# Stores of a last batch issued per 32 rows over two queues, with a new instruction order

## The chip, the core and the metric

The kernel runs on one core of a Trainium2 chip. The metric is the device time of one execution in microseconds, as the median of five executions. A profiled execution gives, beside its own time, the span from its first to its last instruction; what lies between the two is outside the instructions. Engines: TensorE (PE) multiplies matrices and writes to the banks of PSUM; VectorE (DVE) and ScalarE (ACT) copy, add and apply functions; GpSimd (POOL) issues the loads here; SyncE (SP) issues transposing transfers and stores. ScalarE can issue stores too.

## The reference

An attention of the Nyström kind (8 batches, 8 heads, 576 tokens, 64 wide, 32 landmarks), and on its result, as 4608 tokens of 512 values, two dense layers with SiLU between them (2048 inner values):

```python
q_lm = q.reshape(B, H, m, S // m, D).mean(axis=3)      # m = 32 landmarks
k_lm = k.reshape(B, H, m, S // m, D).mean(axis=3)
A, Bm, C = sm(q, k_lm), sm(q_lm, k_lm), sm(q_lm, k)    # scaled softmaxes
Z = Bm.T / (norm(Bm, 1) * norm(Bm, inf) + 1e-06)
for _ in range(6):
    Z = 2 * Z - Z @ Bm @ Z
x = A @ Z @ C @ v                                       # then (B*S, H*D)
...
h = x @ w_in
g = h * (1.0 / (1.0 + np.exp(-h)))
return g @ w_out
```

## The kernel before

**Work of one batch.** The name of an operation ends in its batch (`A.3`). The kernel loads q, k and v of the batch (`ld`, `ldv`), transposes q and k (for batches 0 to 2 on TensorE, `tr` with copies `trc`; for later ones with four transposing transfers on SP, `xt`), and sums over the 18 positions of a landmark (`lms` on TensorE, or the VectorE tree `lra`, `lrb`, `lrc`, `lrd`). `sb` and `pb` make the small softmax, `ns0` to `ns5` on TensorE with `nsd0` to `nsd5` on VectorE the six iterations of the inverse. `A` is the softmax of q against the landmarks: scores `A`, exponentials `Ax`, sums `S`, reciprocals through `Ln` and `Rs`, product `etn`. `C`, `Cx`, `ct` (a transpose) and `cv` make C times v. `zt` multiplies with Z, and `m0` to `m3` multiply that with `w_in` at once, so that layer 1 is one small product, `etn` times `m`: sixteen tiles `h0` to `h15` of 512 tokens, each with a SiLU on ScalarE (`g0` to `g15`), and `hx0`, `hx8` with `gx0`, `gx8` for the 64 tokens left over of the batch. The SiLU needs another function table in ScalarE than the exponentials, and the kernel groups the two kinds.

**Layer 2** takes 256 tokens at a time (`layer2_pair`, from line 1027), in two halves of 128. The 2 x 2 blocks of tokens and columns are made with seven products instead of eight, as in Strassen's scheme: sums of blocks on VectorE (`ss0` to `ss3`), products `p1` to `p7` of eight matmuls each on TensorE, and copies (`c1`, `u2`, `c5`, `c21`) and additions (`c11`, `c22`, `c12`) that bring them into two tiles `ost` of the output, a low one and a high one, each of 128 tokens by 512 columns. Names carry a priority: `p1@5120` is batch 1 (5000 + 100 per batch), second pair (+ 20); + 40 is the pair that gathers the left-over tokens of four batches. The low tile is whole after `c11` (columns 0 to 255) and `c12` (256 to 511), the high one after `c21` and `c22`. There are six `ost` tiles in turn.

**Stores.** One tile of 128 rows is four blocks of 32 rows, which lie 18 rows apart in the output, so it leaves as four transfers (`store`, line 1021). Ordinarily one operation `os` on SP issues all four (line 1118). For the very last pair (`spread`, line 1108), the four stores of the low tile are four operations that SP or ACT may take, and the high tile is stored in eight halves of 256 columns, those of each half as soon as it is made.

**The order.** All is planned ahead: `Plan.run` (line 86) is a list scheduler. It keeps a time for each engine, takes the ready operation with the lowest priority, counts the costs and lags written in the code, and gives for every engine a fixed order of instructions, which the kernel then emits. Where TensorE would idle in the first 45 us of the plan, it issues a matmul on zeros (`P.filler`, line 497). Priorities may be shifted by the table `ORDER` (line 19), `name: (shift, not before)`, which was found by a search. The engines wait for one another through semaphores as the data need it; so an instruction that waits holds up all that stands behind it on its engine.

Of the kernel before, what the change touches and what calls it, by code (L numbers as in the profile page):

```python
# [16 lines left out]


ORDER = {
    "tr09.0": (11.858, 0), "f0.0": (2417.6, 0), "nsd20.0": (1178, 0), "stf1.0": (616.27, 0),  # L20
    "ns51.0": (572.47, 0), "A.0": (-14.244, 0), "Ax10.0": (-14.785, 0), "S10.0": (429.53, 0),
    "Ln10.0": (-9.5622, 0), "etn1.0": (303.1, 0), "mc00.0": (-3617.7, 0), "mc30.0": (2226.2, 0),
    "tr10.1": (11.49, 0), "trc09.1": (-0.41208, 0), "tr014.1": (4003.2, 0), "lms110.1": (600, 0),
    "lms1112.1": (182.03, 0), "lms006.1": (4219.8, 0), "ns00.1": (-205.63, 0),
    "Ax10.1": (-68.603, 0), "Ln10.1": (-2.9831, 0), "Ax11.1": (-215.55, 0),
    "Ln11.1": (-2436.1, 0), "Rs1.1": (-229.25, 0), "Cx00.1": (3739.9, 0), "ctc10.1": (-135.78, 0),
    "trc014.2": (-5.8828, 0), "Ln10.2": (-1553.1, 0), "Cx10.2": (-2.3811, 0), "h11.1": (3839, 0),
    "c12@5100.0": (-2978.9, 0), "A.3": (-178.57, 0), "cv0.3": (-11.245, 0), "h2.2": (332.83, 0),
    "h3.2": (185.78, 0), "h4.2": (18.041, 0), "h11.2": (452.76, 0), "h15.2": (51.328, 0),
    "p5@5200.0": (-179, 0), "c21@5200.0": (912.94, 0), "A.4": (-26.98, 0), "Ln00.4": (288.73, 0),  # L30
    "h11.3": (169.04, 0), "ss00@5320.0": (-3259.3, 0), "p5@5340.0": (-0.29183, 0),
    "p7@5340.0": (-4146.8, 0), "p3@5340.0": (212.88, 0), "nsd00.5": (-245.94, 0),
    "S10.5": (-942.67, 0), "p7@5420.0": (-0.18573, 0), "ns40.6": (267.98, 0),
    "ss00@5500.0": (-5226.2, 0), "cv0.7": (-3352.4, 0), "wrc.7": (1720.5, 0),
    "p5@5620.0": (-0.51334, 0), "p7@5700.0": (-1.908, 0), "p4@5720.0": (524.17, 0),
    "p2@5740.0": (15.37, 0),
}


# [272 lines left out]
def mm_us(n, count=1):  # L312
    return count * max(n / 2400 + 0.0025, 0.028)
# [3 lines left out]
def kernel(  # L317
# [10 lines left out]
    B, H, S, Dh = q.shape  # L328
# [31 lines left out]
    def bank(o, i=0):  # L360
        return banks[o.slot[i]]
# [33 lines left out]
    def mm(out_ap, lhsT, rhs, start=True, stop=True):  # L395
        nc.tensor.matmul(out=out_ap, lhsT=lhsT, rhs=rhs, start=start, stop=stop,  # L396
                         skip_group_check=True)
# [6 lines left out]
    def copy(e, out, in_):  # L404
        if e == "ACT":
            nc.scalar.copy(out=out, in_=in_)  # L406
        elif e == "DVE":
            nc.vector.tensor_copy(out=out, in_=in_)  # L408
        else:
            nc.gpsimd.tensor_copy(out=out, in_=in_)  # L410

    P = Plan()
    A = P.add

    def either(n, act=True, dve=True):
        r = []
        if dve:
            r.append(("DVE", dve_us(n)))
        if act:
            r.append(("ACT", act_us(n)))  # L420
        return r
# [512 lines left out]
    l2_last = {}  # L934
# [56 lines left out]
    ost_st = {}  # L991

    def layer2_plain(gm, c, deps, places, prio):

        pieces = []
        for h in range(2):
            cell = {}
            cols = slice(c + 128 * h, c + 128 * h + 128)
            for qt in range(4):
                def f(e, qt=qt, cell=cell, cols=cols):  # L1000
                    for dc in range(4 * qt, 4 * qt + 4):
                        mm(bank(cell["o"]), gm[:, dc, cols], w_out_sb[:, dc, :], start=(dc == 0),
                           stop=(dc == NDC - 1))
                d = deps(4 * qt, 4 * qt + 4) + [wo_ops[qt]]
                o = A(f"o{qt}@{prio + h}", [("PE", mm_us(512, 4))], f,
                      d + ([(pieces[-1], 0.0)] if qt else []), prio + h + 0.01 * qt,
                      psum=0 if qt else 1, cls="L2")
                cell.setdefault("o", o)
                pieces.append(o)
            i = nost[0] % 6  # L1010
            nost[0] += 1
            t = ost_r[i]
            a = A(f"oc@{prio + h}", either(512), lambda e, t=t, cell=cell: copy(
                e, t, bank(cell["o"])), [pieces[-1]] + ost_st.get(i, []),
                500.0 + prio / 100).reads(cell["o"])
            ost_st[i] = [A(f"os@{prio + h}", [("SP", 2.2)],
                           lambda e, t=t, h=h: [store(e, t, places[h], m) for m in range(4)],
                           [a], prio, dma=0.65, lag=3.5)]
        return pieces

    def store(e, t, place, m, cols=slice(0, DMODEL)):
        b, j = place[m]
        {"SP": nc.sync, "ACT": nc.scalar}[e].dma_start(
            out=out[b * S:(b + 1) * S, cols].rearrange("(l j) n -> j l n", j=J)[j],
            in_=t[L * m:L * m + L, cols])

    def layer2_pair(gm, c, deps, places, prio, parts=1, spread=False):

        n = npair[0]
        npair[0] += 1  # L1030
# [8 lines left out]
        for u in range(parts):  # L1039
            k = slice(w * u, w * u + w)  # L1040
            dep = deps(w * u, w * u + w) + deps(HC + w * u, HC + w * u + w) + ss_last.get(n - 2, [])
            for i, (o_, x, y, op) in enumerate((
# [6 lines left out]
                dep = [a]  # L1049
# [24 lines left out]
        def evac(nm, engs, f, deps, *of):  # L1074
            c = A(f"{nm}@{prio}", engs, f, deps, 500.0 + prio / 100)
            for o in of:
                c.reads(o)
            return c

        def add(out_, x, y):  # L1080
            nc.vector.tensor_tensor(out=out_, in0=x, in1=y, op=OP.add)  # L1081
# [3 lines left out]
        def ps(o):  # L1085
            return bank(o)[:, 0:HM]
# [3 lines left out]
        p2 = prod("p2", 1, a12, b21, [p1] + deps(HC, NDC) + w2)  # L1090
        c1 = evac("c1", half, lambda e: copy(e, lo_t[:, 0:HM], ps(p1)), [p1] + lo_free, p1)
        c11 = evac("c11", dve, lambda e: add(lo_t[:, 0:HM], lo_t[:, 0:HM], ps(p2)), [p2, c1], p2)
        p6 = prod("p6", 2, s2, wt[:, 1], [c1] + sums[2] + wts[1], p1)
        u2 = evac("u2", half, lambda e: copy(e, lo_t[:, HM:DMODEL], ps(p1)), [p6], p1)
        p5 = prod("p5", 3, s1, wt[:, 0], [p1] + sums[0] + wts[0])
        p7 = prod("p7", 4, a21, b12, [u2] + sums[1] + wts[3], p1)
# [3 lines left out]
        p3 = prod("p3", 5, s4, b22, [c5] + sums[3] + w2, p5)  # L1100
        p4 = prod("p4", 6, a22, wt[:, 2], [c22] + wts[2], p1)
        c12 = evac("c12", dve, lambda e: add(lo_t[:, HM:DMODEL], lo_t[:, HM:DMODEL], ps(p5)),
                   [p3, u2], p5)
        c21 = evac("c21", half, lambda e: copy(e, hi_t[:, 0:HM], ps(p1)), [p4], p1)
        ss_last[n] = [p3, p5, p6]

        for i, t, h, dep in ((lo_i, lo_t, 0, [c11, c12]), (hi_i, hi_t, 1, [c21, c22])):
            if spread and h:
                ost_st[i] = [A(f"os{u}{m}@{prio + h}", [("SP", 0.45), ("ACT", 0.45)],
                               lambda e, m=m, t=t, u=u: store(e, t, places[1], m, slice(  # L1110
                                   HM * u, HM * u + HM)), [dep[u]], prio + 0.1 * u,
                               dma=0.1, lag=1.5) for u in range(2) for m in range(4)]
            elif spread:
                ost_st[i] = [A(f"os{m}@{prio}", [("SP", 0.45), ("ACT", 0.45)],
                               lambda e, m=m, t=t: store(e, t, places[0], m), dep, prio,
                               dma=0.1, lag=1.5) for m in range(4)]
            else:
                ost_st[i] = [A(f"os@{prio + h}", [("SP", 2.2)],
                               lambda e, t=t, h=h: [store(e, t, places[h], m) for m in range(4)],
                               dep, prio, dma=0.65, lag=3.5)]  # L1120
        return pieces

    def layer2_batch(b):
        l2_last["m", b] = []
        for p in range(2):
            x = (gm_r[b % 2], 256 * p, lambda d0, d1: gm_ops[b][d0:d1],
                 [[(b, j) for j in range(8 * c + p, 8 * c + p + 7, 2)] for c in range(2)],
                 5000.0 + 100 * b + 20 * p)
            if b or p:
                l2_last["m", b] += layer2_pair(*x)  # L1130
            else:
                l2_last["m", b] += layer2_plain(*x)
                w_sums(l2_last["m", b][:])
        if b % 4 == 3:
            l2_last["x", b // 4] = layer2_pair(
                gx_t, 0, lambda d0, d1: [gx_ops[x][d // 8] for x in range(b - 3, b + 1)
                                         for d in range(d0 // 8 * 8, d1, 8)],
                [[(x, j) for x in (y, y + 1) for j in (J - 2, J - 1)] for y in (b - 3, b - 1)],
                5000.0 + 100 * b + 40, 1, b == B - 1)

    def later_loads(b):
        p = last[b - 2]
# [6 lines left out]
    for b in range(B + 1):  # L1149
        if b < B:  # L1150
            attn(b)
        if b:
            layer1(b - 1)
            layer2_batch(b - 1)
# [53 lines left out]
```

## Time and profile before

| | us |
|---|---|
| five executions | 249.02, 249.9, 249.63, 249.32, 249.56 |
| median | 249.56 |
| the profiled execution | 249.02 |
| its span | 247.3 |
| TensorE busy | 239.0 |
| VectorE, ScalarE busy | 168.7, 180.8 |
| last matmul ends, from the span's start | 242.6 |

The chain of waits and the groups of instructions name lines of the kernel; line 396 is the helper that emits every matmul, 406 and 408 are the copies on ScalarE and VectorE, 958 the SiLU, 1046 the sums of layer 2, 1081 its additions, 1023 a store. A row of a group has the number of instructions, busy time, mean duration of one in ns, and the idle time of the engine before them with what ended it. A matmul's duration overlaps the next one's, so starts tell more than durations. In the timeline a row has start, length, engine, line, what is written from what, the number of instructions merged, and in brackets the idle time before it. The stores' group of the page, with the number of issues, size of one, and the median from issue to landing:

```profile
out_dram<-ost SPq DMA_DIRECT2D x138, 64.0 KB, 1.8
out_dram<-ost SPq DMA_DIRECT2D x4, 32.0 KB, 1.5
out_dram<-ost ACTq DMA_DIRECT2D x4, 32.0 KB, 1.6
out_dram<-ost ACTq DMA_DIRECT2D x2, 64.0 KB, 1.8
```

### The profile page before, as it was taken

Reading aid. Unit: us, or ns where it says so; the run is one execution under the profiler, and the core shown is the slowest. Engines: PE = TensorE matmul, PEld = TensorE weight load, DVE = VectorE, ACT = ScalarE, POOL = GpSimd, SP = SyncE. Lnnn points to the kernel's source line nnn. Section 1 sums busy time; section 2 is a strip of 40 time slices with the busy share of each in tenths; the row PEclk is TensorE's granted clock in tenths of the full one; section 3 lists DMA queues with packets and bytes.
Section 4 is the critical chain, followed back from the end, with each engine's and each line's share of the span. In section 5 each row is a group of like instructions: output and inputs, shape, how many; then the busy total and the mean of one; then the engine's idle time right before and its main releaser. Section 6 shows DMA issues by size and latency. Waiting matters only on the chain.

```text
span 247.3 us, 7085 instructions
## 1 busy us (share of the span) xinstructions
PE 239.0 (97%) x2780; PEld 171.2 (69%) x2780; DVE 168.7 (68%) x432; ACT 180.8 (73%) x443; POOL 37.2 (15%) x63
## 2 busy tenths in 40 slices
PE   7999999999989999999999999999999999999992
PEld 5786664556867645577886645697885665788881
DVE  2379765495979947939998787099988365056620
ACT  2596997499776999999359998868667998831220
POOL 8436823300022004000310050000000000000000
PEclk9999999999999999999999999999999999999999
DMA  6999999999999999989899999884354003032332
GB/s 102 195 203 197 203 207 206 207 242 166 187 133 217 183 136 185 221 140 175 155 248 205 180 175 222 149 148 83 89 120 107 0 3 85 3 85 67 96 95 85
DMA packets 55680, 36.50 MB, mean 148 GB/s; under 512 B 36576, under 2 KB 47072, under 8 KB 55648
## 3 DMA queue, kind: packets, MB, share of 16 engines
q0 software_dynamic: 15264, 18.35, 44.5%
q1 hardware_dynamic: 40096, 17.45, 33.3%
q8 instruction: 21, 0.34, 0.5%
q10 hardware_dynamic: 288, 0.26, 0.4%
q14 instruction: 11, 0.09, 0.1%
HBM read 36.70 MB, written 9.44 MB: 187 GB/s over the span
## 4 chain that ended last, share of the span: by engine, by line
PE 88%; DMA 5%; DVE 2%; ACT 2%; issue 1%; POOL 0%; SPq 0%; DVEq 0%; POOLq 0%
PE ps L396 85%; DMA qk<-in_q_dram 3%; PE ps L570 2%; DMA qT<-qk 2%; ACT gm L958 1%; DMA out_dram<-ost 1%; DVE red L630 1%; PE ps L846 1%; POOL qk L449 0%; DVE ost L1081 0%; DVE ss L1046 0%; DVE gm L1046 0%; ACT pb L695 0%; ACT gx L981 0%; DVE st L756 0%
## 5 line engine op out<-in xcount | busy, mean ns | idle before, releaser
L396 PE MATMUL ps<-etn,m 128*128 128x64 bf16 (+1 forms) x512 | 69.5, 286 | 0.6 <-ACT gm L958 0.6
L958 ACT ACTIVATE gm<-ps 128x512 f16<-128x512 f32 x128 | 66.8, 658 | 1.3 <-PE ps L396 1.1
L396 PEld LDWEIGHTS <-gm 128*128 128x128 f16 x512 | 48.6, 98 | 11.4 <-issue 2.7
L396 PE MATMUL ps<-w_out_sb,gm 128*128 128x256 f16 (+1 forms) x392 | 53.1, 281 | 0.0
L396 PEld LDWEIGHTS <-m 128*128 128x128 bf16 x512 | 32.2, 98 | 24.3 <-issue 2.7
L406 ACT COPY ost<-ps 128x256 f32<-128x256 f32 (+1 forms) x55 | 21.2, 388 | 37.1 <-PE ps L396 34.6
L396 PEld LDWEIGHTS <-ss 128*128 128x128 f16 x408 | 38.8, 98 | 7.8 <-issue 2.3
L1081 DVE TENSOR_TENSOR ost<-ost,ps 128x256 f32<-128x256 f32 x51 | 21.3, 418 | 31.0 <-PE ps L396 24.4
L396 PE MATMUL ps<-wt,ss 128*128 128x256 f16 x272 | 34.3, 273 | 0.7 <-DVE ost L1081 0.7
L756 DVE SCALAR_TENSOR_TENSOR st<-st,ps 128x320 bf16<-128x320 bf16 (+3 forms) x54 | 21.7, 406 | 7.7 <-PE ps L396 6.7
L408 DVE CAST m<-ps 128x512 bf16<-128x512 f32 x31 | 20.1, 686 | 3.5 <-PE ps L396 3.5
L406 ACT CAST m<-ps 128x512 bf16<-128x512 f32 x33 | 18.2, 618 | 1.5 <-PE ps L396 1.4
L396 PE MATMUL ps<-w_out_sb,ss 128*128 128x256 f16 x136 | 17.6, 273 | 0.0
L455 POOL DMA_DIRECT2D qk<-in_k_dram x7 | 5.0, 714 | 79.8 <-DMA ct<-ce 41.4
L462 POOL DMA_DIRECT2D v<-in_v_dram x24 | 14.0, 590 | 15.7 <-PE ps L396 8.8
L396 PE MATMUL ps<-zer 128*128 128x256 bf16 x88 | 15.2, 298 | 1.1 <-DVE zer L489 1.1
L396 PE MATMUL ps<-wt,gm 128*128 128x256 f16 x120 | 15.6, 273 | 0.0
L831 ACT ACTIVATE ce<-ps 128x288 bf16<-128x288 f32 x32 | 12.7, 418 | 3.2 <-PE ps L396 3.2
L396 PE MATMUL ps<-st 128*128 128x160 bf16 (+1 forms) x96 | 14.6, 225 | 0.1
L1046 DVE TENSOR_TENSOR ss<-gm 128x1024 f16<-128x1024 f16 x15 | 10.2, 683 | 4.9 <-ACT gm L958 4.9
L796 ACT ACTIVATE ln<-ps 128x288 f32<-128x288 f32 x32 | 12.0, 433 | 1.8 <-PE ps L396 1.6
L396 PEld LDWEIGHTS <-st 128*128 128x128 bf16 x96 | 8.5, 97 | 6.0 <-issue 1.1
(91 smaller groups left out, 322.1 us busy)
## 6 DMA issues: line engine op xcount, KB each, us to landing
out_dram<-ost SPq DMA_DIRECT2D x138, 64.0 KB, 1.8
v<-in_v_dram POOLq DMA_DIRECT2D x24, 192.0 KB, 11.0
qk<-in_k_dram POOLq DMA_DIRECT2D x7, 576.0 KB, 6.6
qk<-in_q_dram POOLq DMA_DIRECT2D x7, 576.0 KB, 10.1
w_out_sb<-in_moe_w_out_dram POOLq DMA_DIRECT2D x4, 512.0 KB, 10.3
w_in_sb<-in_moe_w_in_dram POOLq DMA_DIRECT2D x4, 256.0 KB, 9.1
w_in_sb<-in_moe_w_in_dram POOLq DMA_DIRECT2D x8, 128.0 KB, 7.4
qk<-in_k_dram POOLq DMA_DIRECT2D x2, 288.0 KB, 4.4
```

The source lines that it names most:

```text
L396: nc.tensor.matmul(out=out_ap, lhsT=lhsT, rhs=rhs, start=start, stop=stop, skip_group_check=True)
L406: nc.scalar.copy(out=out, in_=in_)
L408: nc.vector.tensor_copy(out=out, in_=in_)
L455: lambda e, t=t, src=src: nc.gpsimd.dma_start(out=qk_r[b % 2][:, t].rearrange("p g j d -> p g (j d)"), in_=src[b].rearrange("(g h) (l j) d ...
L462: lambda e, a=a: nc.gpsimd.dma_start(out=v_r[b % 2][a * L:(a + 1) * L, :, :], in_=v[b].rearrange("h (l a x) d -> a l h (x d)", l=L, a=VA)[ ...
L570: nc.tensor.transpose(out=ps[:, n * 128:(n + 1) * 128], in_=qk[:, t, g, 2 * jp:2 * jp + 2, :].rearrange("p j d -> p (j d)"), identity=idb)
L756: nc.vector.scalar_tensor_tensor(out=s2[:, g0:g1, lo:SW], in0=s[:, g0:g1, lo:SW], scalar=2.0, in1=ps[:, 0:NG * SW].rearrange("p (g x) -> p ...
L796: lambda e, g=g, c=c, ln=ln: nc.scalar.activation(out=ln[:, c], in_=bank(me["S", g, c])[:, 0:HS], func=AF.Ln),
L831: nc.scalar.activation(out=ce[:, :, 0:VP].rearrange("p (i c) (a l) -> p c a i l", c=2, a=VA)[:, c], in_=bank(me["C"], 2 * g + c)[:, 0:HS]. ...
L958: lambda e, dc=dc, cell=cell: nc.scalar.activation(out=gm[:, dc, :], in_=bank(cell["o"]), func=AF.Silu),
L1046: lambda e, o_=o_[:, k], x=x[:, k], y=y[:, k], op=op: nc.vector.tensor_tensor(out=o_, in0=x, in1=y, op=op), dep, 850.0 + prio / 100)
L1081: nc.vector.tensor_tensor(out=out_, in0=x, in1=y, op=OP.add)
```

## The change

The two ordinary pairs of the last batch (`@5700`, `@5720`) get `spread` 1: each of their four tiles is stored by four operations that SP or ACT may take. The last pair (`@5740`) gets `spread` 2: both tiles in eight halves. The costs that the planner counts for stores change, and the table of shifts is another one, which gives another order of instructions from the first batch on. No other code changes.

```diff
 ORDER = {
-    "tr09.0": (11.858, 0), "f0.0": (2417.6, 0), "nsd20.0": (1178, 0), "stf1.0": (616.27, 0),
...
-    "p2@5740.0": (15.37, 0),
+    "f0.0": (200.69, 0), "A.0": (-135.46, 12.93), "Ln11.0": (-57.289, 0), "etn1.0": (-31.554, 0),
...
+    "ss00@5500.0": (-5226.2, 0), "p7@5700.0": (633.04, 0), "p4@5720.0": (524.17, 0),
 }
...
-            ost_st[i] = [A(f"os@{prio + h}", [("SP", 2.2)],
+            ost_st[i] = [A(f"os@{prio + h}", [("SP", 2.4)],
...
-    def layer2_pair(gm, c, deps, places, prio, parts=1, spread=False):
+    def layer2_pair(gm, c, deps, places, prio, parts=1, spread=0):
...
-            if spread and h:
-                ost_st[i] = [A(f"os{u}{m}@{prio + h}", [("SP", 0.45), ("ACT", 0.45)],
-                               lambda e, m=m, t=t, u=u: store(e, t, places[1], m, slice(
+            if spread == 2:
+                ost_st[i] = [A(f"os{u}{m}@{prio + h}", [("SP", 0.46), ("ACT", 0.46)],
+                               lambda e, m=m, t=t, u=u, h=h: store(e, t, places[h], m, slice(
                                    HM * u, HM * u + HM)), [dep[u]], prio + 0.1 * u,
                                dma=0.1, lag=1.5) for u in range(2) for m in range(4)]
             elif spread:
-                ost_st[i] = [A(f"os{m}@{prio}", [("SP", 0.45), ("ACT", 0.45)],
-                               lambda e, m=m, t=t: store(e, t, places[0], m), dep, prio,
-                               dma=0.1, lag=1.5) for m in range(4)]
+                ost_st[i] = [A(f"os{m}@{prio + h}", [("SP", 0.66), ("ACT", 0.5)],
+                               lambda e, m=m, t=t, h=h: store(e, t, places[h], m), dep, prio,
+                               dma=0.16, lag=3.0) for m in range(4)]
             else:
-                ost_st[i] = [A(f"os@{prio + h}", [("SP", 2.2)],
+                ost_st[i] = [A(f"os@{prio + h}", [("SP", 2.4)],
...
-                l2_last["m", b] += layer2_pair(*x)
+                l2_last["m", b] += layer2_pair(*x, spread=int(b == B - 1))
...
-                5000.0 + 100 * b + 40, 1, b == B - 1)
+                5000.0 + 100 * b + 40, 1, 2 * (b == B - 1))
```

## The prediction

> **What bounds the kernel now.** I read the page first (busy shares, chain), then who waits for whom on TensorE, then busy time by stretches, then the timeline at the two long waits and at the end. Page and waits:
>
> ```profile
> PE 239.0 (97%) x2780; PEld 171.2 (69%) x2780; DVE 168.7 (68%) x432; ACT 180.8 (73%) x443; POOL 37.2 (15%) x63
> PE 88%; DMA 5%; DVE 2%; ACT 2%; issue 1%; POOL 0%; SPq 0%; DVEq 0%; POOLq 0%
> PE ps L396 <- DVE zer L489: 1.1, 1, 1.1
> PE ps L396 <- DVE ost L1081: 0.7, 1, 0.7
> PE ps L396 <- DMA qk<-in_q_dram: 0.6, 1, 0.6
> PE ps L396 <- ACT gm L958: 0.6, 1, 0.6
> PE ps L396 <- DMA qk<-in_k_dram: 0.3, 1, 0.3
> L396 PE MATMUL ps<-zer 128*128 128x256 bf16 x88 | 15.2, 298 | 1.1 <-DVE zer L489 1.1
> ```
>
> TensorE is the bound: 97% busy, and all its waits sum to 3.3 us. The last row says that 88 of its matmuls are fillers on zeros, issued where the planner found nothing to do; they are waiting in disguise. By stretches (length, then busy us of each engine, clock, DMA share, GB/s):
>
> ```profile
> 12.70:34.40 21.70, 21.58 (x356) 15.55 (x349) 18.77 (x58) 19.08 (x54) 11.89 (x18) 1.00 1.23 201
> 34.40:70.00 35.60, 35.60 (x376) 22.43 (x374) 23.85 (x58) 28.71 (x66) 4.91 (x8) 1.00 1.13 196
> 70.00:72.00 2.00, 1.27 (x13) 0.95 (x12) 1.41 (x4) 1.39 (x5) 0.38 (x1) 1.00 0.95 205
> 86.00:90.00 4.00, 3.43 (x33) 1.93 (x32) 2.68 (x6) 3.97 (x7) 0.00 (x0) 1.00 0.66 142
> 90.00:205.00 115.00, 114.87 (x1344) 81.02 (x1343) 88.11 (x221) 95.64 (x235) 9.40 (x15) 1.00 0.76 143
> 205.00:242.60 37.60, 37.58 (x316) 30.36 (x311) 16.00 (x31) 16.12 (x38) 0.00 (x0) 1.00 0.28 73
> 242.60:247.40 4.80, 0.00 (x0) 0.00 (x0) 0.42 (x1) 0.00 (x0) 0.00 (x0) 0.93 0.28 82
> ```
>
> From 90 to 242.6 us TensorE idles 0.15 us in all: a new order has nothing to win there. Three places are left: the fillers before 34.4 us, the waits at 71 and 88 us, and the 4.7 us after the last matmul. The timeline there:
>
> ```profile
> 70.59 0.69 DVE L630 TENSOR_TENSOR red<-qT 128x1024 f16<-128x1024 bf16 x1 [1.37 <-DMA qT<-qk]
> 71.67 1.03 PE L396 MATMUL ps<-wt,ss 128*128 128x256 f16 x8 [0.73 <-DVE ost L1081]
> 86.45 1.28 ACT L958 ACT_TABLE_LOAD   x1
> 88.39 1.00 PE L396 MATMUL ps<-etn,m 128*128 128x512 bf16 x14 [0.57 <-ACT gm L958]
> 242.62 0.42 DVE L1081 TENSOR_TENSOR ost<-ost,ps 128x256 f32<-128x256 f32 x1 [1.32 <-PE ps L396]
> 243.74 0.78 SPq L1023 DMA_DIRECT2D out_dram<-ost  x2
> DMA to landing us min/median/max: 1.8/1.8/1.9
> ```
>
> (The last line is that of the two stores above it.) At 71 us VectorE waits for a transpose of q and TensorE waits behind it. At 88 us ScalarE has just loaded the SiLU table. After the last matmul come an addition, full-row stores behind half-row ones, and a landing.
>
> **What the skill says.** "DMA: Bandwidth & Descriptors", section "Issuing engines are not separate DMA queues": a second issuing queue saves only issue time. The trace agrees that there is something to save: a store occupies SP for 0.31 to 0.45 us, while the DMA share of the last stretches is 0.28. The same page, "Anatomy of one DMA": a semaphore wait is held at the issuing sequencer, and most of a transfer's fixed cost is the write's receipt. Here 64 KB land in 1.8 us and 32 KB in 1.5, so halving a store gains 0.2 to 0.3 us, not half. "ScalarE: Activation LUTs", "Rules for kernel authors", budgets about 2.7 us for a change of table; this trace shows 1.28 us, which I use. "TensorE: Matmul & The Clock Gate", "Wait — 56ns, not 53.3ns?", gives N/2.4 GHz + 2.5 ns: 109 ns for 256 columns, 0.873 us for a product of eight; the windows give 37.58 us for 316 matmuls of mixed width. TensorE cannot be made faster, only less idle.
>
> **The change part by part.** The order of both programs shows the same matmuls, except 79 fillers instead of 88, and 12 table loads instead of 8. The sums are against the profiled execution: span 247.3 us, time 249.02 us, the lowest of the five; the median 249.56 lies 0.54 above it.
>
> *Fillers and the start.* The first 42 fillers stand as before. After these there are 37 instead of 46; a filler takes 0.109 us start to start, so 9 x 0.109 = 1.0 us. The ScalarE queue agrees: between the second batch's pb and the SiLU load it loses the copies ctc00.1 (0.74) and ztc.0 (0.26), again 1.0 us. Against it, both etn products now stand before stf0.0 on VectorE, which starts the first Newton-Schulz chain about 1.2 us later; the two halves then alternate instead of trailing each other. I take 0.8 us earlier at 35 us (bounds 0 and 1.3), but it does not survive as such:
>
> *The pin at 70.6 us.* Loads keep their order and move about 200 GB/s from 12.7 to 70 us, so they land when they did. The fourth transpose of batch 3 lands at 70.5 and lra0.3 starts at 70.59 whatever TensorE has done. Behind it on VectorE stand, in both orders, c11@5100, lrb0.3, nsd00.2 (0.69, 0.41, 0.42, 0.48, slightly overlapped), and nsd00.2 ends at 72.35. Before, TensorE stops at p5@5100, which needs c11. Now p5@5100 and p7@5100 come ahead and it stops at ns10.2, about 1.4 us, until 72.4. After that both orders hold the same work up to A.3: ns10.2 0.14, p3 0.87, cv0.2 0.79, ns20.2 0.14, ltr0.3 0.11, p1 0.87, ns30.2 0.14, sb.3 0.11, p4 0.87, and 0.2 for changes of tile shape, 4.2 us. A.3 starts at 76.65; before 77.17, with small waits between. **-0.5 us** (bounds -1.0, +0.3).
>
> *The SiLU load at 86 to 88 us.* Then the fifth tile of layer 1 waited 0.73 us for g0.2. Now p4@5120 (0.97 with its change of shape) stands behind m3.2: TensorE has 0.34 + 0.43 + 0.15 + 0.97 + 3 x 0.43 + 0.14 = 3.3 us of work before that tile, ScalarE three copies at 0.48, the load 1.28 and the first SiLU 0.6, also 3.3 us. A remainder of 0.3 us is taken for lags: **-0.4 us** (bounds -0.7, 0).
>
> *Four more table loads.* gx8.3 and gx8.5 were left out of their SiLU groups and each gets a load there and one back, 2 x 1.28 us plus 0.6 of ScalarE. Each stands where TensorE has layer-2 products. After gx8.3 the copy c1@5300 is needed by p6@5300, and between p1 and p6 lie ltr, p4, p2, cv, ns20, 2.8 us; I find the copy some 1.9 us early. Around gx8.5, c1@5500 is some 0.6 us early and C.7 to A.7 tight but covered. **0** (bounds 0, +2).
>
> *New waits from 90 to 242 us.* Nothing to win: **+0.1** (bounds 0, +1.5). In the last two full pairs the stores move from SP alone to SP and ACT: ACT issues 16 stores instead of 6, some 0.4 us each, 4 us more, in a stretch of 37.6 us of which it is busy 16.1. There they wait for VectorE's additions with copies behind them (u2@5720 and c1@5720 among these); each copy is needed a product (0.87 us) or more after it could be made, so 0 (bounds -0.1, +0.5). Nobody waits for these stores themselves. The new constants for a store (2.4 for 2.2 and the like) only steer the planner.
>
> *The end.* With T the end of the last matmul: before, the addition ends at T + 0.46, but eight stores for each half stand close, SP waits for a store's landing, and its last issue starts at T + 1.5 and lands at T + 3.35. Now the last products are p7, p3, p4, each 0.87, and their results leave in groups of four half stores, two on each queue: c22's at T - 1.25, c12's at T - 0.37, c21's at T + 0.51 and, 0.46 later, T + 0.97 (or at T + 0.75 at the earliest if a landing is waited for, which hides). A second half store took up to 1.7 us to land: T + 2.7. **-0.65 us** (bounds -0.9, -0.2). The 1.4 us from the last landing to the span's end stay.
>
> Sum: -0.5 - 0.4 + 0 + 0.1 - 0.65 = -1.45. Span 245.85, execution 247.57, at the median 249.56 - 1.45 = **248.1 us**.
>
> **Rivals.** *Only the tail.* The transposes' pin eats the start, and small waits return what the two places give: -0.65, 248.9. For it: the pin is DMA's. Against: the order around both waits did change.
> *Given back.* New waits of 0.9 to 1.9 us between 90 and 205, where the old order had none: 249.1 to 250.0. For it: 115 us with 0.13 us of idle time can only get worse.
> *Slower: the added table loads.* If ScalarE runs over 1.9 us late at gx8.3 and 0.6 at gx8.5 then p6@5300, p6@5500 and A.7 wait behind loads. With half of the two detours (2 x 3.2 us) uncovered TensorE loses 3.2, net +1.75: 251.3; it decides from a loss of 2 us on. For it: ScalarE is 83% busy from 90 to 205. Against: three to five products lie over each.
>
> **Chances.** Forecast 62% (246.9 to 248.9), only the tail 12%, given back 8%, slower 18%. A measurement tells about 0.2%, 0.5 us, from no change. Faster 0.62 + three quarters of 12% = 0.71; same 0.03 + 0.08 = 0.11; slower 0.18. The range 246.9 to 250.2 adds up the good bounds partly and cuts off the worst of the slow case.
>
> **What would show it.** Right: last matmul to span's end about 4.1 us instead of 4.7; TensorE's wait near 71 us longer and before a 128x160 matmul; the wait at 88 us halved; no idle over 0.3 us after 90. Wrong: a TensorE wait for ScalarE near 118 or 178 us, a busy time from 90 to 205 that leaves over 1 us idle, or a last store that lands over 3 us after the last matmul.

## The result and the profile after

| | before | changed | changed, measured again |
|---|---|---|---|
| median, us | 249.56 | 248.43 | 247.86 |
| ratio to before on the same chip, 95% interval | | 0.9948 [0.9929, 0.9967] | 0.9931 [0.9910, 0.9953] |
| profiled execution, us | 249.02 | 247.97 | 247.86 |
| its span | 247.30 | 246.14 | 246.03 |
| A.3 starts | 77.17 | 76.08 | 75.82 |
| zt.3 starts | 94.95 | 93.27 | 93.02 |
| m0.3 starts | 96.02 | 95.87 | 95.75 |
| h0.3 starts | 99.26 | 99.04 | 98.92 |
| p1@5700 starts | 218.84 | 218.66 | 218.54 |
| last matmul ends (T) | 242.58 | 242.40 | 242.29 |
| last store issued, T plus | 1.52 | 1.12 | 1.13 |
| last store landed, T plus | 3.35 | 2.76 | 2.77 |
| last landing to the span's end | 1.38 | 0.98 | 0.98 |

The starts are those of each operation's first matmul in the profiled execution. The changed kernel is 0.5 to 0.7% faster. The rows show how the lead of the changed kernel grows and goes: 1.1 us at A.3, 1.7 at zt.3, 0.15 at m0.3, then 0.2 to the last matmul, and 1.0 more behind it. The page of the changed kernel (line numbers are 2 lower than before): busy times, chain, and the row of the fillers:

```profile
PE 238.5 (97%) x2771; PEld 170.5 (69%) x2771; DVE 171.8 (70%) x441; ACT 183.5 (75%) x438; POOL 37.3 (15%) x63
PE 73%; DMA 16%; ACT 3%; POOL 3%; DVE 1%; issue 1%; SPq 1%; POOLq 0%; DVEq 0%
...
L394 PE MATMUL ps<-zer 128*128 128x256 bf16 x79 | 14.2, 301 | 1.1 <-DVE zer L487 1.1
```

And what TensorE waited for (us in total, times, longest):

```profile
PE ps L394 <- DVE zer L487: 1.1, 1, 1.1
PE ps L394 <- DMA qk<-in_q_dram: 1.0, 1, 1.0
PE ps L394 <- DVE zt L406: 1.0, 1, 1.0
PE ps L394 <- ACT gm L956: 0.4, 1, 0.4
```

The chain runs through transfers for 16% of the span, since behind the new wait stands a transpose and, further back, loads; TensorE is busy for 97% as before. The wait for VectorE's `ost` at 71 us is gone, that for the SiLU (`gm`) is smaller, and a wait of 1.0 us for `zt` is new. The wait for q, at 9 us, precedes everything and moves with the landing of that load. The nine fillers fewer are as announced. The stretches with idle time at stake:

```profile
70.00:72.00 2.00, 2.00 (x22) 1.76 (x21) 2.00 (x7) 1.79 (x6) 0.00 (x0) 1.00 0.95 93
86.00:90.00 4.00, 3.61 (x31) 1.89 (x29) 2.14 (x6) 3.99 (x9) 0.00 (x0) 1.00 0.47 106
90.00:205.00 115.00, 114.01 (x1348) 80.78 (x1345) 89.20 (x223) 98.45 (x233) 9.44 (x15) 1.00 0.77 146
205.00:242.40 37.40, 37.40 (x312) 30.20 (x309) 18.61 (x36) 14.32 (x33) 0.00 (x0) 1.00 0.26 70
```

TensorE (the first number after the comma) is full from 70 to 72 us now and has 0.99 us of idle time between 90 and 205, where it had 0.13. The timeline of the changed kernel at the places that answer to those shown of before, and at the new wait:

```profile
69.36 0.68 DVE L628 TENSOR_TENSOR red<-qT 128x1024 f16<-128x1024 bf16 x1
...
85.28 1.28 ACT L956 ACT_TABLE_LOAD   x1
...
87.22 0.59 PE L394 MATMUL ps<-etn,m 128*128 128x512 bf16 x2 [0.39 <-ACT gm L956]
...
94.78 0.69 DVE L628 TENSOR_TENSOR red<-qT 128x1024 f16<-128x1024 bf16 x1 [2.29 <-DMA qT<-qk]
95.39 0.42 DVE L406 CAST zt<-ps 128x256 bf16<-128x256 f32 x1
...
95.87 0.62 PE L394 MATMUL ps<-w_in_sb,zt 64*32 64x512 bf16 x16 [0.99 <-DVE zt L406]
...
242.08 1.79 SPq L1021 DMA_DIRECT2D out_dram<-ost  x4
...
242.44 0.42 DVE L406 COPY ost<-ps 128x256 f32<-128x256 f32 x1 [0.45 <-PE ps L394]
```

First row: lra0.3 starts at 69.4 without a wait; its transposing transfer landed at 69.1, not 70.5. The view of the four transposes of batch 3 shows it too, first before, then changed:

```profile
DMA to landing us min/median/max: 3.3/3.4/5.0
DMA to landing us min/median/max: 3.3/3.4/3.5
```

Rows four to six are one chain. VectorE stands idle for 2.29 us at lra1.4, the sum over a half of batch 4, until the transpose of that half lands. Behind lra1.4 stands ztc.3, the copy of zt.3, done by ScalarE before and by VectorE now; and m0.3 on TensorE needs ztc.3. In the kernel before, the same sum stood at the same place but with nothing urgent behind it:

```profile
94.04 0.69 DVE L630 TENSOR_TENSOR red<-qT 128x1024 f16<-128x1024 bf16 x1
```

The transpose that lra1.4 needs was issued at 89.98 (before: 89.28) and landed at 94.69 (before: 93.94). So a TensorE that came 1.7 us earlier met a transfer that did not.

**Why transposes land late.** The page counts transfers of a kind of its own:

```profile
q8 instruction: 21, 0.34, 0.5%
```

The trace has each of these 21: one packet of 16 KB that takes 0.9 to 1.7 us. All 13 profiles together (before, changed and the eleven experiments below) have 260 transposes of q and k. In 170 of them no such packet started between 1 us before and 3.3 us after the issue, and all 170 landed 3.2 to 3.5 us after it. In the other 90 one did, and 87 landed after 4.0 to 5.5 us. Before, such a packet started at 68.45, 0.4 us before the fourth transpose of batch 3 would have landed by its usual 3.4 us; in the changed kernel one started at 69.11, with the landing at 69.14. The transpose that lra1.4 waits for was delayed by one in both kernels (at 91.0 and 91.7). No experiment moves these packets, so that they cause the delay is inferred from how cleanly the cases split.

### The profile page after: what moved, and what is told of

Same layout as the page of the kernel before. It is cut to its first block, busy times and chain, and to the rows that moved or that the text cites. A ratio compares the mean times of both kernels' runs of the same rounds, so it can differ in the third digit from the quotient of the medians.

```text
span 246.1 us, 7075 instructions
## 1 busy us (share of the span) xinstructions
PE 238.5 (97%) x2771; PEld 170.5 (69%) x2771; DVE 171.8 (70%) x441; ACT 183.5 (75%) x438; POOL 37.3 (15%) x63
## 4 chain that ended last, share of the span: by engine, by line
PE 73%; DMA 16%; ACT 3%; POOL 3%; DVE 1%; issue 1%; SPq 1%; POOLq 0%; DVEq 0%
PE ps L394 72%; DMA v<-in_v_dram 11%; DMA w_in_sb<-in_moe_w_in_dram 3%; DMA qT<-qk 2%; POOL qk L447 1%; PE ps L568 1%; ACT m L404 1%; POOL v L460 1%; ACT gm L956 1%; POOL w_out_sb L477 1%; POOL qk L453 1%; ACT ce L829 1%; SPq L592 1%; ACT L956 1%; ACT ln L794 0%
## 5 line engine op out<-in xcount | busy, mean ns | idle before, releaser
L394 PE MATMUL ps<-etn,m 128*128 128x512 bf16 (+1 forms) x512 | 68.9, 286 | 0.4 <-ACT gm L956 0.4
L956 ACT ACTIVATE gm<-ps 128x512 f16<-128x512 f32 x128 | 66.1, 652 | 2.0 <-PE ps L394 1.8
L404 ACT COPY ost<-ps 128x256 f32<-128x256 f32 (+1 forms) x48 | 18.4, 383 | 37.6 <-PE ps L394 30.5
L406 DVE COPY ost<-ps 128x256 f32<-128x256 f32 x22 | 9.3, 423 | 15.0 <-PE ps L394 14.2
L394 PE MATMUL ps<-zer 128*128 128x256 bf16 x79 | 14.2, 301 | 1.1 <-DVE zer L487 1.1
L404 ACT COPY qT<-ps 128x640 bf16<-128x640 bf16 (+1 forms) x12 | 7.9, 691 | 6.0 <-PE ps L568 6.0
```

Of the source, the lines that this page charges most:

```text
L956: lambda e, dc=dc, cell=cell: nc.scalar.activation(out=gm[:, dc, :], in_=bank(cell["o"]), func=AF.Silu),
```

## The experiments

All replay a written order of instructions (`engine:operation`, with a `!` where a table is loaded first), so that no instruction moves but those in the diff. All compute the whole of the reference.

**The two halves of the change.** The kernel is cut at p4@5600, near 209 us: one takes the old order up to there and the new end, the other the new order up to there and the old end.

```diff
-first part: order of before          second part: end of before
+first part: order of before          second part: end of changed   (end alone)
+first part: order of changed         second part: end of before    (order alone)
```

> The order of before up to the product p4@5600 and from there the order and the stores of the changed kernel. If the end alone carries the gain (my reading): the last matmul ends at about 242.6 us as before, the last store lands some 2.75 us after it instead of 3.35, and the time is 0.6 to 1.0 us under before (about 248.8). If the new order carries it (rival): 0 to 0.2 us under before.

> The order of the changed kernel up to p4@5600 and from there the order and the stores of before. My reading: the last matmul ends 0.2 us earlier than before (242.4), the tail is the old one (4.7 us), the time is 0.2 us under before (about 249.4), not to be told from it. Rival, that the order brings most of the gain: 0.8 us or more under before.

Measured: the end alone 248.91 us, 0.9968 [0.9949, 0.9987]; the order alone 248.94, 0.9957 [0.9934, 0.9979]. Both halves gain, 0.8 and 1.1 us at 249.7, and about add up to the whole (1.3 and 1.7 in its two measurements). For the order it is the rival's outcome that came, not my 0.2. In the profile of the order alone TensorE ends at 241.80 and the last store lands 3.37 us later, as before; the end alone ends at 242.50 and lands 3.60 later, with two issues of 1.26 and 1.35 us at 241.7 in place of 0.42. A 16 KB packet of the instruction kind started at 241.3 in that execution. So it shows the mechanism of the end badly; the four experiments on stores below show it better.

**The new wait taken away.** Only lra1.4 moves, behind ztc.3.

```diff
 SP:os@5120.0
-DVE:lra1.4
 ACT:g14.2
...
 DVE:ztc.3
+DVE:lra1.4
 PE:h3.2
```

> The changed kernel with one VectorE instruction moved: the copy ztc.3 stands ahead of lra1.4, which waits for a transpose, instead of behind it. If the lead that TensorE had at 93 us is lost at this copy alone: m0.3 starts at about 94.8 instead of 95.9, the wait of 1.0 us for zt goes, and TensorE's end and the time fall by 0.8 to 1.1 us below the changed kernel (about 247.5). If loads and transposes hold TensorE anyway (rival): another wait takes its place within 20 us and the time falls by 0.2 us or less.

Measured: 248.19 us, 0.9931 [0.9908, 0.9954]; the changed kernel's interval covers it. TensorE's timeline of this kernel:

```profile
94.75 0.62 PE L591 MATMUL ps<-w_in_sb,zt 64*32 64x512 bf16 x16
95.31 1.05 PE L591 MATMUL ps<-w_out_sb,gm 128*128 128x256 f16 x8
97.18 0.63 PE L591 MATMUL ps<-w_in_sb,zt 64*32 64x512 bf16 x16 [0.82 <-DVE m L603]
```

m0.3 starts at 94.75 instead of 95.87, so the reading of the 0.99 us was right. But 0.82 us come back at once: m2.3 waits for VectorE's copies of m0.3, which stand behind the rest of the same tree. h0.3 starts at 98.77, 0.27 earlier than in the changed kernel. Moving the copies ahead of the tree too gave no more (only the new places of the moved operations are shown):

```diff
 DVE:mc10.3
+DVE:lra1.4
+DVE:lrb1.4
...
 DVE:mc31.3
+DVE:lrc1.4
+DVE:lrd1.4
+DVE:lra0.4
...
 PE:h1.3
+PE:ltr1.4
 ACT:g0.3
+ACT:lmT1.4
```

> The changed kernel with what waits for the transposes of batch 4 moved out of the way: on VectorE ztc.3, mc00.3 and mc10.3 stand ahead of lra1.4 and lrb1.4, and mc21.3 and mc31.3 ahead of lrc1.4, lrd1.4 and lra0.4; ltr1.4 follows h1.3 on TensorE and lmT1.4 follows g0.3 on ScalarE. If VectorE's queue behind the transpose is the whole of the second pin: no wait of TensorE over 0.3 us between 90 and 110 us, h0.3 about 1 us earlier than in the changed kernel, TensorE's end and the time 0.8 to 1.0 us below it (about 247.5). If a later transfer pins TensorE again (rival): h0.3 1 us earlier, but C.5 or p1@5600 within 0.3 us of the changed kernel.

Measured: 248.03 us, 0.9936 [0.9913, 0.9959]. No idle time near 95 or 97, but 0.44 us at 101.1, where ltr1.4 waits for the tree's last sum. Its profiled execution took 249.59, 1.6 above its median, with a wait of 1.78 at 73.0 behind a late transpose, so its starts are not compared with others. But within it TensorE needs only 4.67 us from zt.3 to h0.3 (changed: 5.77) and then 120.6 from h0.3 to p1@5700 (changed: 119.6): what is won near 96 us is given back, most of it before 106 us. VectorE's work around the late transpose has to be done somewhere before 101 us.

**Is the lead of the start worth anything?** Eight fillers more, ahead of h6.0.

```diff
 ACT:g3.0
+PE:warm  (8 times)
 PE:h6.0
```

> The changed kernel with eight more filler matmuls ahead of tile h6.0, 8 x 0.109 = 0.87 us more of TensorE time at 34 us. If leads and lags of the start are lost at the waits near 70 and 95 us (my reading): h0.1 starts 0.9 us later, the wait of 1.0 us for zt at 95 us shrinks to 0.3 or less, m0.3 starts within 0.2 us of where it did, and the time is within 0.3 us of the changed kernel (248.4). If TensorE's sum of work sets the time (rival): 0.87 us more (249.3).

Measured: 248.73 us, 0.9941 [0.9920, 0.9961], not to be told from the changed kernel. In the profile h0.1 starts 0.71 later than in the changed kernel, A.3 1.58 later (the transpose landed at 70.97 in this execution), m0.3 0.52 later (0.2 was expected) and h0.3 0.48. Waits of 0.51 at 72.9 and 0.17 at 76.4 came, that at 96 us went: idle time moved from one place to the other.

**The SiLU groups.** gx8.3 and gx8.5 go back into their groups: 8 table loads instead of 12.

```diff
 ACT:g15.3
+ACT:gx8.3
 ACT:pb.4!
...
-ACT:gx8.3!
...
-ACT:pb.5!
+ACT:pb.5
...
 ACT:gx0.5
+ACT:gx8.5
...
-ACT:gx8.5!
...
-ACT:Cx00.7!
+ACT:Cx00.7
```

> The changed kernel with gx8.3 and gx8.5 put back into their SiLU groups: 8 table loads instead of 12, ScalarE some 5 us less busy. If the four added loads are covered by TensorE's products (my reading): TensorE's end and the time as the changed kernel's, within 0.3 us. If they cost (rival): the time falls by 0.5 us or more below the changed kernel.

Measured: 249.33 us, 0.9970 [0.9952, 0.9989], 0.5 to 1.0 slower than the changed kernel by the ratios, with intervals that touch or overlap; the profile says more. From h0.3 to p1@5700 TensorE takes 119.62 us in the changed kernel and in every kernel that keeps its order there, to 0.01 us; here it takes 120.61, about half of the loss near 111 us, behind gx8.3, and half near 166 us, behind gx8.5. So the added loads are no cost but a gain of 1.0 us within this order. ScalarE's timeline at the second place, first of the changed kernel, then of this one:

```profile
162.81 1.08 ACT L979 ACTIVATE gx<-ps 128x512 f16<-128x512 f32 x2
163.90 1.28 ACT L1159 ACT_TABLE_LOAD   x1
165.20 0.89 ACT L693 ACTIVATE pb<-ps 32x64 f32<-32x64 f32 x4
```

```profile
162.66 2.06 ACT L1176 ACTIVATE gx<-ps 128x512 f16<-128x512 f32 x4 [0.97 <-PE ps L591]
164.73 1.28 ACT L1356 ACT_TABLE_LOAD   x1
166.03 0.90 ACT L890 ACTIVATE pb<-ps 32x64 f32<-32x64 f32 x4
```

And a line of TensorE's waits in this kernel, which the changed one doesn't have:

```profile
PE ps L591 <- ACT pb L890: 0.3, 1, 0.3
```

gx8.5's two SiLU calls, some 1.0 us, stand ahead of the load and of the exponentials pb, so pb starts 0.83 later and TensorE waits. Left out, they cost two loads of 1.28 us later, where a product covers them. The order of before keeps the groups and needs 119.58 from h0.3 to p1@5700 in two of its three profiles (in the third 120.7, with VectorE waiting for late transposes near 146 us): it paid nothing there either, having the work arranged in another way.

**The low tile of the last pair in whole rows.** Order of the last products as in the changed kernel; four stores of 64 KB after c12 in place of eight of 32 KB.

```diff
-ACT:os00@5740.0  SP:os01@5740.0  ACT:os02@5740.0  SP:os03@5740.0
 PE:p5@5740.0
...
-ACT:os10@5740.0  SP:os11@5740.0
+ACT:os0@5740.0  SP:os1@5740.0  ACT:os2@5740.0  SP:os3@5740.0
 DVE:c21@5740.0
-ACT:os12@5740.0  SP:os13@5740.0
```

> The changed kernel and its order, but the low tile of the last pair stored in four whole rows after c12, as before the change, instead of in eight halves. If the order of the last products (p4 last, p2 early) is what shortens the end: the last issue starts at 1.1 us and the last store lands at 2.75 us after the last matmul, as in the changed kernel, and the time is the same within 0.2 us. If the halves of the low tile shorten it: the last store lands at 3.3 us and the time is 0.5 us longer.

Measured: 248.94 us, 0.9961 [0.9941, 0.9981]. Last issue T + 1.10, last landing T + 3.02, closing 1.23 (changed: 1.12, 2.76, 0.98). So the halves are worth 0.26 of landing, and of the 0.59 by which the change shortened it the rest is there without them. The times alone do not tell this kernel from the changed one; the reading rests on the profile.

**Halves in the old order.** Before's order, but the low tile in halves, and c21 on VectorE.

```diff
+ACT:os10@5740.0  SP:os11@5740.0  ACT:os12@5740.0  SP:os13@5740.0
 PE:p2@5740.0
-ACT:c21@5740.0
+DVE:c21@5740.0
...
 DVE:c11@5740.0
-ACT:os0@5740.0  SP:os1@5740.0  ACT:os2@5740.0  SP:os3@5740.0
+ACT:os00@5740.0  SP:os01@5740.0  ACT:os02@5740.0  SP:os03@5740.0
```

> The kernel before and its order, with the low tile of the last pair in eight halves, those of c12 issued before the last product, and the copy c21@5740 on VectorE instead of ScalarE. If either cure is enough for the end (my reading): the last issue starts at 1.1 us instead of 1.5 and the last store lands at 2.7 to 2.8 us after the last matmul instead of 3.35, and the time falls by 0.5 us below before. If only the new order helps (rival): 3.3 us and no change.

Measured: 250.40 us, 1.0033 [1.0012, 1.0053]: slower than before. Last issue T + 2.80, last landing T + 4.36. The end shows waits of SP's queue. SP's waits from 205 us on, of before, of this kernel, and of the changed kernel (where stores are line 1021; it has no such line, and the one shown is the closing wait):

```profile
SPq L1023 <- DMA out_dram<-ost: 1.5, 2, 1.3
```

```profile
SPq L1217 <- DMA out_dram<-ost: 2.2, 3, 1.7
```

```profile
SPq L1201 <- DMA out_dram<-ost: 0.9, 3, 0.4
```

The records of the transfers name the semaphore that each landing will raise. There are eight (111 to 118) for all stores and transposes of both queues, used again and again, and a store is held at its queue until the earlier transfer with its semaphore has landed:

```
                  waits for the semaphore of   which ACT issued   landed    SP issues
before            118                          240.94             242.58    242.65
before            113                          242.20             243.68    243.74
old order, halves 118                          241.56             243.13    243.15
all full rows SP  112                          241.91             243.59    243.60
```

(The last row belongs to the next experiment.) The queue that comes late waits for a store that the other has only just issued. The longest wait isn't always the one that counts. In the kernel before the half tile that the store with 118 carries is made by 242.18 only, so 118 holds it back by 0.45 us of the 1.3; and the semaphore 113 keeps SP's last two stores until 243.7 whatever came earlier, 0.64 us after their half is made (242.62 + 0.42). In the old order with halves SP waits four times in a row (118, 112, 114, 115) for landings of stores that ACT issued some 1.55 us earlier, the last until 244.60, and three more issues follow. The end behind the last matmul is 0.55 us longer than before (4.36 + 0.92 against 3.35 + 1.38); that TensorE ends 0.6 us later in this profile too comes from near 146 us, where the order is that of before. In the changed kernel ACT's stores raise only 111, 113, 115 and 117, and SP's last ones only the other four; so each queue meets semaphores of its own, and SP never waits.

**All stores on SP, in two steps.** First only the sixteen full-row stores of the two ordinary pairs, then all 32 of the last batch.

```diff
-ACT:os0@5700.0  SP:os1@5700.0  SP:os2@5700.0  ACT:os3@5700.0
+SP:os0@5700.0  SP:os1@5700.0  SP:os2@5700.0  SP:os3@5700.0
 (and so @5701, @5720, @5721; in the second kernel @5740, @5741 too)
```

> The changed kernel with the sixteen full-row stores of the last batch's two ordinary pairs all on SP; the end of the last pair stays as it is on both queues. Theory (nobody waits for these stores, and SP has done them by 241 us at 0.42 us each): no difference from the changed kernel, 0.0 us, between -0.3 and +0.3; last issue +1.1 and last landing +2.75 us after the last matmul. Rival (SP comes late into the last pair, so spreading the full pairs over two queues is worth something by itself): last issue +1.6 us or later, +0.4 us or more.

> The changed kernel with all 32 stores of the last batch's three pairs on SP, none on ScalarE; the order and the halves stay. Theory (issuing is what limits the end: twelve half stores from the next-to-last addition on, 0.42 us each, one queue instead of two): the last issue starts 11 x 0.42 = 4.6 us after the first of them instead of 2.3, so it is 3.4 us after the last matmul instead of 1.1, the last landing 5.0 instead of 2.75, and the median 2.3 us above the changed kernel (1.8 to 2.6). Rival (the transfers share one set of DMA engines and finish no earlier for being issued on two queues): +0.8 us or less, and landings that come sooner after their issue, 1.0 to 1.2 us.

Both are compared with the changed kernel measured again (247.86). The full rows on SP: 250.14 us, 1.0001 [0.9974, 1.0027], 1.75 above the changed kernel by the ratios. Last issue T + 3.53, last landing T + 5.09. The theory fell: nobody waits for these stores, but the last pair's stand behind them. SP issues without a pause from 235.4 to 239.9, then waits twice, 2.4 us together, for landings of ScalarE's stores:

```profile
SPq L1218 <- DMA out_dram<-ost: 2.4, 2, 1.4
```

All on SP: 251.96 us, 1.0069 [1.0039, 1.0100], 3.4 above the changed kernel by the ratios. Last issue T + 5.12, last landing T + 6.68. No wait for a landing, but no pause either, in SP's timeline, and the view of these stores for their landings:

```profile
235.69 12.92 SPq L1218 DMA_DIRECT2D out_dram<-ost  x28
```

```profile
DMA to landing us min/median/max: 1.5/1.6/1.7
```

28 issues in 12.92 us are 0.46 each. The expectation counted only the last twelve and was 1.7 us short. The landing after an issue is what it was on two queues, so the transfers don't hinder one another: what bounds the end is issuing. The Trainium skill, "DMA: Bandwidth & Descriptors", section "Issuing engines are not separate DMA queues", says that a second issuing engine saves only the time to initiate, which is usually small beside the transfer. That it saves only issuing fits these landings; but here this is 3.9 us of the last landing (6.68 against 2.76), as 28 small stores stand close together.

**The changed kernel once more**, as a control.

> The changed kernel with its own order of instructions, nothing altered: a second profile and a second measure of it. Theory (where the start and the transposes of batch 3 fall differs by half a microsecond from execution to execution, the rest is fixed by the program): the same median within 0.3 us of 248.4, TensorE's waits of 0.4 us near 87 us and of 0.7 to 1.2 us near 96 us in place again, the last store issued 1.1 us and landed 2.75 us after the last matmul. Rival (the wait near 96 us was an accident of one execution): none over 0.3 us there, and TensorE's end at 241.5 us or earlier.

Measured: 247.86 us, 0.9931 [0.9910, 0.9953], with waits of 0.40 us at 87.0 and 1.13 at 95.7, and the end as in the first table. The new wait is no accident of one execution: of the seven profiles that keep the changed order up to h0.3, six have it, with 1.0 to 1.7 us. In these six the transpose of lra1.4 landed 4.6 to 4.9 us after its issue, and h0.3 started 4.35 us after that landing, to 0.01 us; in the seventh (full rows on SP) it landed after 3.5 us.

## Why the prediction was right, and where not

The forecast of 248.1 us stands 0.3 below one median and 0.2 above the other. Its sum was made of other parts than the ones that came, so that it came out this close is in part luck.

- *Fillers and the start*: "does not survive" was right, and sooner than said: of the lead of 0.8 us expected at 35 us, 0.30 is there at h15.0 (39.64 against 39.94), where both orders have done the same work again, and 0.09 at zt.1 (46.83 against 46.92).
- *The pin at 70.6 us, -0.5*: the place was right, the fixed time not, and **the gain was not there**. The transpose landed at 69.14 in the changed kernel, 68.49 in its repeat, 70.47 before, and A.3 came 1.09 earlier. But where the fourth transpose landed as late in the new order (70.83 to 71.09: eight fillers, the later tree, full rows on SP), A.3 followed 6.69 us after the landing, against 6.70 in the kernel before: with an equal landing the new order wins nothing. TensorE's work from its stop to A.3 takes 4.76 us in these three, where the sum had 4.2. The earlier A.3 (76.17 on average over the seven profiles that keep the new order up to h0.3, 76.98 over three with the old) goes with the earlier landing. Late landings were three of three with the old order and three of ten with the new, too few to say whether the order makes them rarer. The sign that was named, a longer wait near 71 us, was not seen in either profile of the changed kernel; where the transpose came late it was, in full rows on SP with 1.7 us at 72.8.
- *The SiLU load, -0.4*: the wait fell from 0.57 to 0.39, so 0.2.
- *Four more table loads, 0*: from h0.3 to p1@5700 119.62 us against 119.58: right. Its bounds were on one side only: within the new order the added loads gain 1.0.
- *New waits from 90, +0.1*: **this step failed.** The stretch was called one where there was "nothing to win", its waits were bounded by 1.5, and the likeliest value was put at nearly nothing. It cost 1.0 in the profile: ztc.3, moved from ScalarE to VectorE, was not followed to what stands ahead of it there, a sum that waits for a transpose. At m0.3 the lead of 1.7 us is down to 0.15. Over the same ten profiles h0.3 starts at 99.17 on average with the new order and at 99.07 with the old: the middle gives nothing that these profiles can show, in place of -0.8. The rival "given back" had this mechanism, at 8%.
- *The stores of the ordinary pairs, 0*: right for TensorE. Read as "these stores don't matter" it is wrong: on SP alone they make the end 2.3 us later.
- *The end, -0.65*: -0.59, of which 0.26 is from the halves and the rest from the order of the last products, with SP's waits for landings gone. The last products of before start 0.87 us apart (239.80, 240.67, 241.54), as the sum took them. What the prediction quotes on the make-up of a transfer's fixed cost stands on its page under transfers issued by GpSimd; these stores are issued by SP and ACT, and no run here takes their cost apart. The 1.4 us after the last landing didn't "stay": 0.98, another -0.4. At its end SP waits for the semaphores in the order of their numbers, and each one left costs 0.06 us: from the last landing to the end of these waits it takes 0.29 us where 114 landed last (before) and 0.11 where 117 did (changed). What follows takes 0.87 to 0.98 us in twelve of the 13 profiles and 1.09 in that of before. So about 0.2 of the 0.4 is the program's, and 0.2 is that one execution.

So the right total is a middle of about nothing instead of -0.8 and an end of -0.8 to -1.0 instead of -0.65. One thing stays open: the order alone measured -1.1 [-1.6, -0.5] by its ratio, the profiles give it 0 before 219 us, with starts of h0.3 that spread from 98.4 to 99.8 for the same order. What the order is worth, and by what, these runs don't settle.

## What to carry to other kernels

When a copy moves to another engine, look at what is ahead of it in that queue and what that waits for; a transfer's landing there holds everything behind it, and gains made earlier are lost at the first such place. Before a start that came earlier is put down to an order, look whether the transfer it waits for landed earlier by itself. At a program's end count the issues that are left per queue, from the point where the queue has no more pauses, not only the last few. With two queues keep them in step, as a store may have to wait for the other queue's latest landing.

## What was not expected of the hardware

- Eight semaphores shared by the stores and transposes of both queues, so that one queue's issue waits for the other's landing: waits of 1.3 us at the end of the kernel before, 1.7 and 1.4 in two experiments. The instructions themselves name the semaphore, so this belongs to the program as it was built.
- The last transpose of batch 3 landed between 68.5 and 71.1 us, 3.4 to 5.5 us after its issue. It was late in the six profiles where a 16 KB packet of the instruction kind started at least 0.38 us before the landing was due (3.4 us after the issue), and in time in the seven where the packet started 0.03 us before that or later.
- In each profile some stores far from the end were slow: near 228 us one issue took 1.53 us (changed), 1.43 and 1.73 (the two kernels with stores on SP) instead of 0.42, and stores around it landed 2.7 to 3.2 us after their issue in these three instead of 1.7. Every profile has one of the 16 KB packets there, between 226.7 and 229.5 us. TensorE waited for none of these stores.
